# Thresholds of eight pairs through DRAM, weights from another queue, eight score buffers and new task ranks in a fused attention and feed-forward kernel

## The chip, the cores and the metric

One core of one Trainium2 chip. In the profile lines TensorE is PE, VectorE DVE, ScalarE ACT and GpSimd POOL; SP is the engine that here does nothing but issue loads and stores. A load is issued by an engine into that engine's own DMA queue (q1 is SP's, q0 POOL's, q10 ScalarE's). The metric is the device time of one execution in microseconds, as the median of several executions. A ratio is the mean time of one kernel's fast runs over that of the kernel before in the same rounds, so it is not quite the ratio of the medians that stand beside it. The span in a profile is about 2 us shorter than the device time of the same execution.

## The reference

Attention over q, k and v of shape 8 x 8 x 576 x 64 (batch, heads, sequence, head size). A score stays only if it is within `tau` of its row's maximum; the rest is masked:

```python
scores = scale * np.matmul(q, k.transpose(0, 1, 3, 2))
thresh = np.max(scores, axis=-1, keepdims=True) - tau
scores = np.where(scores >= thresh, scores, -1000000000.0)
scores = scores - np.max(scores, axis=-1, keepdims=True)
attn = np.exp(scores)
attn = attn / (np.sum(attn, axis=-1, keepdims=True) + 1e-09)
x = np.matmul(attn, v)
```

Its output, as 4608 tokens of 512, goes through a feed-forward layer: `h = x @ w_in` (512 x 2048), `g = h * sigmoid(1.702 h)`, `g @ w_out` (2048 x 512). The weights arrive in double precision.

## The kernel before

Heads are taken two at a time: 32 pairs, four to a batch, numbered 0 to 31. The feed-forward layer runs in nine blocks of 512 tokens; block 0 needs pairs 0 to 3 and, from its first product on, the converted weights. "hps" is the first product of a block (with `w_in`), "ops" the second (with `w_out`), "ps" are scores, "pv" weighted values, "den" sums. A small list scheduler in the kernel file gives every task an engine, a cost and a rank, and fixes each engine's instruction order when the kernel is built; on the chip every engine runs its list in order.

A 64-bit weight piece (128 x 512) is loaded twice, once shifted by three bytes, into four "stages" in the space of the later `w_out` or into two spare buffers; VectorE and ScalarE turn it into fp32 in four steps:

```python
def load_w(i):                       # 32 pieces, 2 x 512 KB each
    ...
    nc.sync.dma_start(out=t..., in_=dram.bitcast(U32))
    nc.sync.dma_start(out=t3...[:, 0 : 8 * WC - 3], in_=dram.bitcast(U8)[:, 3 : 8 * WC])
...
a = task("SP", 1.1, rank, load_w, i, take=place, lag=5.0)
e = task("DVE", 0.44, rank, cv_ex, i, after=[a])
m = task("ACT", 0.72, rank, cv_power, i, after=[e])
a = task("DVE", 1.14, rank, cv_frac, i, after=[e])
...                                   # and cv_end on DVE
```

A pair's row maxima are reduced on VectorE, lowered by `tau`, and spread over 128 partitions by one wide transpose. They are then subtracted from the scaled scores:

```python
def spread_max(n):
    mb = home(n, "mb", 2 * S, "mb", 1)
    nc.vector.transpose(out=mb, in_=stats[n, ALU.max].unsqueeze(2).to_broadcast([P, 2 * QB, 32]))

def sub(n, t):
    nc.vector.scalar_tensor_tensor(
        out=s, in0=s, scalar=scl, in1=mb, op0=ALU.mult, op1=ALU.subtract)
    # the last 64 keys: two instructions of half the width, one a head

def exps(n, t):
    nc.scalar.activation(out=s, in_=s, func=AF.Exp, bias=shift)
```

Of the kernel before, what the change touches and what calls it, by code (L numbers as in the profile page):

```python
# [19 lines left out]
P = 128  # L20
GELU_SCALE = 1.702
EPS = 1e-9

# [6 lines left out]
def kernel(  # L30
# [48 lines left out]
    work = ctx.enter_context(tc.tile_pool(name="work", bufs=2))  # L79
    psA = ctx.enter_context(tc.tile_pool(name="psA", bufs=3, space=bass.MemoryType.PSUM))  # L80
# [6 lines left out]
    kd = [const.tile([P, P], FP32, name=f"kd{i}") for i in range(2)]  # L87
# [4 lines left out]
    tau_b = const.tile([P, 1], FP32, name="tau_b")  # L92
    scl = const.tile([P, 1], FP32, name="scl")
    shift = const.tile([P, 1], FP32, name="shift")
# [6 lines left out]
    limits = {"psA": 3, "psM": 2, "s_m": 7, "s_t": 2, "io": 3, "xT": 3, "mb": 1,  # L101
              "raw0": 1, "raw1": 1, "qkT0": 1, "qkT1": 1, "v_m": 2, "w64": 2}
# [3 lines left out]

    def task(engine, cost, rank, f, *a, after=(), take=(), give=(), lag=0.06):
        tasks.append((engine, cost, rank, f, a, [x for x in after if x is not None],
                      take, give, lag))
        return len(tasks) - 1  # L110

# [117 lines left out]
    def load_w(i):  # L229
        dst, src, c, j = pieces[i]  # L230
        dram = src[ts(c, P), ts(j, WC)]
        if not wide:
            nc.sync.dma_start(out=dst[:, c, ts(j, WC)], in_=dram)
            return
# [12 lines left out]
        nc.sync.dma_start(out=t.rearrange("p c w -> p (c w)"), in_=dram.bitcast(U32))  # L247
        nc.sync.dma_start(
# [41 lines left out]
    mats, sT, stats, mbs, pss = {}, {}, {}, {}, {}  # L290
# [7 lines left out]
    def prep_kd(n):  # L298
        for h in range(2):
            nc.scalar.copy(  # L300
                out=kd[n % 2][ts(h, D), ts(h, D)], in_=mats[n, 1][ts(h, D), MAIN:S]
            )
# [4 lines left out]
    def scores(n, t, c):  # L307
        qT, kT = mats[n, 0], mats[n, 1]
        ps = psA.tile([P, 2, 512], FP32, name="ps", tag="ps")
        if t == NKT:  # L310
            for i in range(2):
                nc.tensor.matmul(  # L312
                    ps[:, i, 0:SH], lhsT=kd[n % 2], rhs=qT[:, ts(i, SH)],
                    start=True, stop=True,
                )
# [10 lines left out]
    def keep(n, t, c):  # L326
# [3 lines left out]
        else:  # L330
            if c == 0:
                st = home(n, "s_m", 2 * S, "s_m", 7, f"s_m{t}")
                st = st.rearrange("p (h s) -> p h s", h=2)
            else:
                st = sT[n, t]
# [4 lines left out]
    def in_groups(n, t, op):  # L340

        if (n, op) not in stats:
            stats[n, op] = [
                work.tile([P, NKT, 2 * QB], FP32, name="part", tag="part", bufs=2),
                work.tile([P, QB], FP32, name="part_t", tag="part_t", bufs=3),
# [8 lines left out]
    def over_tiles(n, op):  # L354

        pm, pt = stats[n, op]
        r = work.tile([P, 2 * QB], FP32, name="red", tag="red", bufs=3)
# [8 lines left out]
    def over_groups(n, op):  # L366
        r = stats[n, op]
        o = work.tile([64, 2 * QB], FP32, name="fold", tag="fold")
# [4 lines left out]
    def lower(n):  # L373
# [3 lines left out]
            out=f[0:32], in0=stats[n, ALU.max][0:32], scalar1=scl[0:32],  # L377
            scalar2=tau_b[0:32], op0=ALU.mult, op1=ALU.subtract,
# [3 lines left out]
        stats[n, ALU.max] = f  # L382

# [6 lines left out]

    def sub(n, t):
        mb, s = mbs[n], sT[n, t]
        if t < NKT:
            nc.vector.scalar_tensor_tensor(  # L394
                out=s, in0=s, scalar=scl, in1=mb, op0=ALU.mult, op1=ALU.subtract
            )
        else:
            for h in range(2):
                x = s[ts(h, D)]
                nc.vector.scalar_tensor_tensor(  # L400
                    out=x, in0=x, scalar=scl[ts(h, D)], in1=mb[ts(h, D), h, :],
                    op0=ALU.mult, op1=ALU.subtract,
# [6 lines left out]
    def exps(n, t):  # L409
        s = sT[n, t]  # L410
        nc.scalar.activation(out=s, in_=s, func=AF.Exp, bias=shift)  # L411
# [58 lines left out]
    def spread_sums(n):  # L470
# [3 lines left out]
        rc = work.tile([P, S], FP32, name="rc", tag="rc")  # L474
# [35 lines left out]
    def tanh(j):  # L510
        ths[j] = work.tile([P, BLK], FP32, name="th", tag="io", bufs=3)
# [16 lines left out]
    def half(i):  # L528
        osbs[i] = work.tile([P, d_model], FP32, name="osb", tag="io", bufs=3)
# [8 lines left out]
    nc.sync.dma_start(  # L538
        out=tau_b, in_=bass.AP(tensor=tau.tensor, offset=tau.offset, ap=[[0, P], [1, 1]])
    )  # L540
    for t in kd + v_t + [ones_t]:
        nc.gpsimd.memset(t, 0.0)
    nc.gpsimd.memset(ones, 1.0)
    nc.gpsimd.memset(rebias, -896.0 * 2.0**23)
    for h in range(2):
        nc.gpsimd.memset(ones_t[ts(h, D), h, :], 1.0)

    def tau_terms():



        nc.vector.tensor_scalar(
            out=scl, in0=tau_b, scalar1=0.0, scalar2=SCALE, op0=ALU.is_ge, op1=ALU.mult
# [4 lines left out]
        nc.vector.tensor_single_scalar(out=shift, in_=tau_b, scalar=-1.0, op=ALU.mult)  # L558




    FIRST, LAST = -1.0, 1000.0
    BY_PE = 5
    LEAD = 6

    ready_w = []
    for i in range(len(pieces)):
        rank = NPAIR - 0.4 + 0.5 * i / n_in if i < n_in else NPAIR - 0.16 + 0.9 * (i / n_in - 1)
        if not wide:  # L570
            ready_w.append(task("SP", 0.6, rank, load_w, i, lag=2.5))
# [3 lines left out]
        a = task("SP", 1.1, rank, load_w, i, take=place, lag=5.0)  # L575
        e = task("DVE", 0.44, rank, cv_ex, i, after=[a])
        m = task("ACT", 0.72, rank, cv_power, i, after=[e])
# [3 lines left out]
        ready_w.append(task("DVE", 0.72, rank, cv_end, i, after=[a, m] + over, give=place))  # L581

    tau_done = task("DVE", 1.0, -2.0, tau_terms)


# [3 lines left out]
    def feed_forward(blk):  # L589
        b = -(-(blk + 1) * BLK // S) - 1  # L590
        xs = [placed[n] for n in range(NPAIR * (b + 1))]
        for j in range(NFC):
            for p in range(2):
                after = ffn[-1:] + xs[-NPAIR:]
                if blk == 0:
# [3 lines left out]
                    "PE", 1.79, LAST, mm1, blk, j, p, after=after,  # L599
# [4 lines left out]
                "DVE", 0.7, FIRST, gelu, j, after=[a, last_mm2.get(j // 2)],  # L604
                give=("psM", "io"),
            )
        for i in range(BLK // P):
            for p in range(NFC // 2):
                after = ffn[-1:] + [gelus[2 * p], gelus[2 * p + 1]]
                if blk == 0:  # L610
# [3 lines left out]
                    "PE", 1.79, LAST, mm2, i, p, after=after, take=("psM",) if p == 0 else (),  # L614
# [10 lines left out]
    for n in range(NP):  # L625
        gate = per_pair * (n - LEAD)
        after = ffn[gate : gate + 1] if gate >= 0 else []
        r = float(n)
        q0, q1 = (nc.sync, nc.scalar) if n == 0 else (nc.sync, nc.sync)
# [106 lines left out]
```

## Time and profile before

| | us |
|---|---|
| time, median of 3 | 1447.86 |
| span of the profiled run | 1446.5 |
| first hps starts | 115.5 |
| last conversion of `w_out` ends | 216.3 |
| block 1 starts (its first hps) | 304.9 |
| from there to the end | 1141.6 |

The lines that carry this stand in the prediction below. Two more views are needed later. The first is what SP's queue issued in the first 20 us (start, duration, then what is loaded where): four loads of pair 1's q take 2.2 us to issue, its k as long, and the first weight piece comes only after the q and k of pairs 0 to 2.

```profile
6.64 2.20 SPq L189 DMA_DIRECT2D gT<-in_q_dram  x4
8.89 2.12 SPq L189 DMA_DIRECT2D gT<-in_k_dram  x4
...
17.77 0.50 SPq L247 DMA_DIRECT2D w_out<-in_moe_w_in_dram  x1
```

The second is what the DMA queues moved between 10 and 16 us (packets, MB, share of the 16 DMA engines): one queue alone, in packets of some 150 bytes, 0.79 MB in 6 us or 130 GB/s.

```profile
q1 hardware_dynamic: 5148, 0.79, 72.3%
```

### The profile page before, as it was taken

The page shows a single profiled execution, that of the slowest core. Times are in us where ns is not written, and L with a number is a line of the kernel's source. Part 1 is how long each engine was busy: PE and PEld are TensorE (multiplying, and loading weights), DVE is VectorE, ACT ScalarE, POOL GpSimd, SP SyncE. Part 2 cuts the span into 40 slices and gives each one's busy share as a digit, 9 for nine tenths or more (in the row PEclk, how much of TensorE's full clock was granted, in tenths as well). Part 3 has the DMA queues.
Part 4 walks back from the last instruction along what each step waited for, and adds up shares of the span by engine and source line. Part 5 has one row for each costly group of instructions (what it writes and reads, how often), then busy time and mean ns, then how long its engine had stood idle before and what let it go on. Part 6 is the DMA issues. An engine that isn't in the chain of part 4 may idle for free.

```text
span 1446.5 us, 13628 instructions
## 1 busy us (share of the span) xinstructions
PE 1384.0 (96%) x4936; PEld 650.1 (45%) x4936; DVE 997.7 (69%) x1650; ACT 643.6 (44%) x885; POOL 1.3 (0%) x13
## 2 busy tenths in 40 slices
PE   5769979899999999999999999999999999999998
PEld 3334434344444444444444444444444444444443
DVE  7998998888978888888878886788777820200100
ACT  5675544555545554555555554455445500100100
POOL 0000000000000000000000000000000000000000
PEclk8879999999999999999999999999999999999999
DMA  8239461111122012211111111111110000000000
GB/s 240 49 130 287 146 251 40 40 25 25 27 44 49 15 29 39 47 32 25 25 40 39 25 25 39 40 25 21 32 36 16 1 7 22 0 7 22 0 7 22
DMA packets 205074, 72.18 MB, mean 50 GB/s; under 512 B 192208, under 2 KB 192208, under 8 KB 205008
## 3 DMA queue, kind: packets, MB, share of 16 engines
q1 hardware_dynamic: 202640, 71.03, 19.1%
q8 instruction: 39, 0.64, 0.2%
q10 hardware_dynamic: 2368, 0.30, 0.1%
q14 instruction: 27, 0.22, 0.1%
HBM read 61.85 MB, written 9.44 MB: 49 GB/s over the span
## 4 chain that ended last, share of the span: by engine, by line
PE 88%; DVE 8%; ACT 1%; DMA 1%; issue 1%; DVEq 0%; ACTq 0%; SPq 0%
PE ops L523 33%; PE hps L504 31%; PE pv L425 11%; PE ps L319 9%; PE ps L312 2%; PE den L425 2%; DVE part L352 1%; DVE s_m L394 1%; DMA w64s<-in_moe_w_out_dram 1%; DVE mb L386 1%; DVE gT L515 0%; DVE w_out L284 0%; DVE w64s L276 0%; DVE part_t L352 0%; ACT s_m L338 0%
## 5 line engine op out<-in xcount | busy, mean ns | idle before, releaser
L523 PE MATMUL ops<-w_out,gT 128*128 128x512 f32 x1152 | 507.0, 597 | 7.4 <-DVE w_out L284 7.3
L504 PE MATMUL hps<-xT,w_in 128*128 128x512 f32 x1152 | 507.6, 596 | 1.5 <-DVE gT L515 1.4
L352 DVE TRANSPOSE_TENSOR_REDUCE part<-s_m 128x36 f32<-128x1152 f32 x228 | 301.3, 1355 | 107.4 <-ACT s_m L338 106.5
L523 PEld LDWEIGHTS ops<-w_out,gT 128*128 128x128 f32 x1152 | 217.7, 191 | 278.6 <-issue 265.7
L504 PEld LDWEIGHTS hps<-xT,w_in 128*128 128x128 f32 x1152 | 215.3, 190 | 274.2 <-issue 244.4
L515 DVE SCALAR_TENSOR_TENSOR gT<-th,hps 128x512 f32<-128x512 f32 x144 | 97.2, 675 | 226.4 <-ACT th L512 225.8
L338 ACT COPY s_m<-ps 128x576 f32<-128x576 f32 x240 | 137.2, 657 | 144.5 <-PE ps L319 143.3
L407 ACT ACTIVATE s_m<-s_m 128x1152 f32<-128x1152 f32 x120 | 138.4, 1153 | 119.7 <-DVE s_m L394 119.6
L512 ACT ACTIVATE th<-hps 128x512 f32<-128x512 f32 x144 | 85.3, 592 | 229.6 <-PE hps L504 229.5
L394 DVE SCALAR_TENSOR_TENSOR s_m<-s_m,scl,mb 128x1152 f32<-128x1152 f32 x120 | 163.3, 1411 | 0.6
L319 PE MATMUL ps<-qkT 64*128 64x288 f32 x960 | 141.8, 433 | 17.3 <-DVE qkT L295 17.3
L411 ACT ACTIVATE s_m<-s_m,shift 128x1152 f32<-128x1152 f32 x120 | 150.2, 1252 | 2.5
L425 PE MATMUL pv<-s_m,v_m 128*64 128x288 f32 x960 | 126.2, 414 | 0.0
L319 PEld LDWEIGHTS ps<-qkT 64*128 64x128 f32 x960 | 83.2, 190 | 89.4 <-issue 40.4
L530 ACT ACTIVATE osb<-ops 128x512 f32<-128x512 f32 x36 | 21.3, 591 | 220.4 <-PE ops L523 220.4
L425 PEld LDWEIGHTS pv<-s_m,v_m 128*64 128x64 f32 x960 | 67.5, 139 | 64.2 <-issue 15.0
L400 DVE SCALAR_TENSOR_TENSOR s_t<-s_t,scl,mb 64x576 f32<-64x576 f32 x60 | 48.7, 812 | 0.4
L492 DVE TENSOR_TENSOR xT<-pv,rc 128x288 f32<-128x288 f32 (+8 forms) x96 | 28.4, 351 | 22.4 <-PE pv L425 21.1
L352 DVE TRANSPOSE_TENSOR_REDUCE part_t<-s_t 128x18 f32<-128x576 f32 x59 | 43.7, 741 | 0.0
L386 DVE STREAM_TRANSPOSE mb<-thr 128x1152 f32<-128x1152 f32 x30 | 41.3, 1377 | 0.9
L312 PE MATMUL ps<-qkT,kd 128*128 128x288 f32 x120 | 37.1, 432 | 0.0
L425 PE MATMUL pv<-s_t,v_t 128*64 128x288 f32 x256 | 36.5, 406 | 0.0
(66 smaller groups left out, 571.1 us busy)
## 6 DMA issues: line engine op xcount, KB each, us to landing
out_dram<-osb SPq DMA_DIRECT2D x36, 256.0 KB, 2.0
q_raw<-in_q_dram SPq DMA_DIRECT2D x120, 72.0 KB, 2.3
k_raw<-in_k_dram SPq DMA_DIRECT2D x116, 72.0 KB, 2.3
v_m<-in_v_dram SPq DMA_DIRECT2D x64, 128.0 KB, 2.4
w_out<-in_moe_w_in_dram SPq DMA_DIRECT2D x12, 512.0 KB, 6.5
w<-in_moe_w_out_dram SPq DMA_DIRECT2D x12, 512.0 KB, 5.0
w_out<-in_moe_w_in_dram SPq DMA_DIRECT2D x12, 511.6 KB, 7.4
w64s<-in_moe_w_out_dram SPq DMA_DIRECT2D x12, 511.6 KB, 6.0
```

Source lines behind the costliest of these rows:

```text
L312: nc.tensor.matmul(ps[:, i, 0:SH], lhsT=kd[n % 2], rhs=qT[:, ts(i, SH)], start=True, stop=True,)
L319: nc.tensor.matmul(ps[:, h, 0:SH], lhsT=kT[ts(h, D), ts(t, P)], rhs=qT[ts(h, D), ts(c, SH)], start=True, stop=True,)
L338: nc.scalar.copy(out=o, in_=pss.pop((n, t, c))[:, :, 0:SH])
L352: nc.vector.tensor_reduce(out=o, in_=i, axis=AXL.X, op=op, apply_transpose=True)
L394: nc.vector.scalar_tensor_tensor(out=s, in0=s, scalar=scl, in1=mb, op0=ALU.mult, op1=ALU.subtract)
L407: nc.scalar.activation(out=s, in_=s, func=AF.Prelu, alpha=STEEP)
L411: nc.scalar.activation(out=s, in_=s, func=AF.Exp, bias=shift)
L425: nc.tensor.matmul(o[c][ts(h, D), 0:SH], lhsT=lhsT, rhs=rhs, start=(t == 0), stop=(t == NKT),)
L504: nc.tensor.matmul(hidden[j], lhsT=w_in[:, c, ts(j, P)], rhs=xTs[blk][:, c, :], start=(c == 0), stop=(c == NDC - 1),)
L512: nc.scalar.activation(out=ths[j], in_=hidden[j], func=AF.Tanh, scale=GELU_SCALE / 2)
L515: nc.vector.scalar_tensor_tensor(out=gT[j], in0=ths.pop(j), scalar=1.0, in1=hidden.pop(j), op0=ALU.add, op1=ALU.mult)
L523: nc.tensor.matmul(acc[i], lhsT=gT[j][:, ts(i, P)], rhs=w_out[:, j, :], start=(j == 0), stop=(j == NFC - 1),)
```

## The change

Its intent: take work off VectorE, whose queue decides when block 0 gets its inputs. For pairs 0 to 7 the thresholds are no longer spread on VectorE. One small transpose brings them into rows of 32 queries, SP writes them to DRAM and reads them back broadcast over the partitions; the scale moves from the subtraction into the exponential. Weights are loaded from POOL's queue, there are eight score buffers instead of seven (paid for with one `kd`, two io buffers and single small ones), the tau load moves to POOL's queue ahead of the weights, the activation table is loaded first, and each kind of task gets its own rank offset.

```diff
-    limits = {"psA": 3, "psM": 2, "s_m": 7, "s_t": 2, "io": 3, ...
+    limits = {"psA": 3, "psM": 2, "s_m": 8, "s_t": 2, "io": 2, ... "mbt": 1, "row": 1, "kd": 1}
+    EARLY = {"lower_rows": -1.16, "values": 0.42, "exps": 0.63, "load_qk": -0.91, "prep": -1.45,
+             "load_v": 0.65, "over_groups": -1.04, "sub": -0.29}       # pairs 0 to 7
+    LATER = {"in_groups": 0.38}                                        # the others
...
-        nc.sync.dma_start(out=t..., in_=dram.bitcast(U32))             # and the shifted copy
+        nc.gpsimd.dma_start(out=t..., in_=dram.bitcast(U32))
...
+    def lower_rows(n):
+        f, o = flat                                                    # 32 x 64 each
+        nc.vector.tensor_scalar(out=f..., in0=stats[n, ALU.max][0:32]..., scalar1=gap[0:32],
+                                scalar2=None, op0=ALU.subtract)
+        nc.vector.transpose(out=o, in_=f)
+    def row_out(n):
+        nc.sync.dma_start(out=rows[n]..., in_=flat[1][0:QB]...)
+    def row_in(n):
+        nc.sync.dma_start(out=mb, in_=row.to_broadcast([P, 2 * S]))
+        for h in range(2):
+            nc.sync.dma_start(out=mbt[ts(h, D)], in_=row[:, ts(h, S)].to_broadcast([D, S]))
...
-            nc.vector.scalar_tensor_tensor(out=s, in0=s, scalar=scl, in1=mb, ...)
+            nc.vector.tensor_tensor(out=s, in0=s, in1=mb, op=ALU.subtract)
...
-        nc.scalar.activation(out=s, in_=s, func=AF.Exp, bias=shift)
+        nc.scalar.activation(out=s, in_=s, func=AF.Exp, scale=scl, bias=shift)
...
+    BY_DMA = 8
-        rank = NPAIR - 0.4 + 0.5 * i / n_in if i < n_in else ...       # weight pieces
+        rank = 3.61 + 0.42 * i / n_in if i < n_in else ...
-        a = task("SP", 1.1, rank, load_w, i, take=place, lag=5.0)
+        a = task("POOL", 2.4, rank, load_w, i, take=place, lag=5.0)
... (smaller cuts of buffers, an earlier rank for cv_end, and cost estimates of the scheduler, left out)
```

## The prediction

> **What bounds the kernel now.** I read the page first (busy shares, slices), then busy time by stage, then what TensorE waited for, then the costliest groups.
>
> ```profile
> span 1446.5 us, 13628 instructions
> PE 1384.0 (96%) x4936; PEld 650.1 (45%) x4936; DVE 997.7 (69%) x1650; ACT 643.6 (44%) x885; POOL 1.3 (0%) x13
> ...
> PE   5769979899999999999999999999999999999998
> ...
> DVE  7998998888978888888878886788777820200100
> ...
> PEclk8879999999999999999999999999999999999999
> ```
>
> TensorE is the bound over the whole span, but the slices below 9 all lie in the first eight (and the very last). Busy time by stage says where the loss ends (columns: stretch, its length, then busy us of PE, PEld, DVE, ACT, POOL with instruction counts, granted clock, DMA share, GB/s):
>
> ```profile
> 0.00:16.00 16.00, 7.75 (x36) 5.10 (x36) 6.35 (x9) 6.75 (x12) 1.34 (x13) 1.00 0.70 122
> 16.00:41.00 25.00, 15.32 (x100) 8.33 (x100) 23.45 (x42) 16.38 (x22) 0.00 (x0) 0.80 0.93 292
> 41.00:118.00 77.00, 54.46 (x338) 28.81 (x335) 72.22 (x121) 50.63 (x63) 0.00 (x0) 0.82 0.37 115
> 118.00:217.00 99.00, 90.12 (x306) 40.71 (x305) 91.79 (x161) 51.10 (x74) 0.00 (x0) 0.97 0.67 220
> 217.00:305.00 88.00, 78.61 (x327) 38.51 (x326) 72.09 (x119) 46.13 (x63) 0.00 (x0) 0.92 0.20 43
> 305.00:1447.00 1142.00, 1137.70 (x3837) 528.68 (x3835) 731.74 (x1204) 472.65 (x654) 0.00 (x0) 1.00 0.12 25
> ```
>
> After 305 us TensorE is always busy at clock 1.00: nothing done for another engine can shorten that part. All 62 us of idle TensorE, and the slow clock, lie before 305, where VectorE is busy 94% of 16:118 and 93% of 118:217. The waits of TensorE name who was late (total, times, longest):
>
> ```profile
> PE ps L319 <- DVE qkT L295: 17.3, 2, 9.4
> PE den L425 <- ACT s_m L411: 16.9, 2, 9.7
> PE den L425 <- ACT gT L411: 14.5, 2, 10.5
> PE ops L523 <- DVE w_out L284: 7.3, 2, 6.3
> ```
>
> The exponentials (L411) wait for VectorE's subtraction, and the other two lines are VectorE itself: its queue sets when block 0's weights and pairs 0 to 7 are ready. In time order, the first product with w_in (hps) starts at 115.5, TensorE waits for the last w_out piece until 216.4 and for the transposes of pair 8 until 292.6, and block 1 starts at 304.9.
>
> **How much TensorE work lies before block 1.** A product of 128x512 costs two instructions of 0.44 us (507 us over 1152), so 0.88. In the timeline the scores of a pair take 5.5 us, its values 5.0, its sums 4.95. Before block 1 lie 128 products (112.8), scores of nine pairs (49.5), values of eight (40) and sums of five (24.8): 227 us of work in 305 us. The changed order of TensorE has exactly the same list before its first product of block 1. So the change is worth what it moves that one moment: span after = start of block 1 + (1446.5 - 304.9 = 1141.6).
>
> **What the Trainium skill says.** "VectorE: DVE Perf Modes", section on the TRN2 errata, gives an fp32 tensor_tensor as (N+151)/0.96 ns: 1357 ns for 1152 columns, 757 for 576. The trace agrees in form: the 128x288 product with rc takes 452 ns. "DMA: Bandwidth & Descriptors", section "Anatomy of one DMA", puts about 2 us of fixed cost on a transfer; here small loads land in 2.1 to 2.7 us. Its section "Issuing engines are not separate DMA queues" says that all queues run on the same 16 DMA engines and interleave: moving the weights to POOL adds no bandwidth. The trace has one case: q on SP and k on ACT together moved 206 GB/s at 3 to 6 us, one queue alone later some 130, with landing 3.6 us instead of 2.3. "TensorE: Matmul & The Clock Gate", section "What's actually happening", says that idle windows throttle the array; here 18 products after the 6.3 us wait took 10.3 us instead of 7.9.
>
> **The change part by part.** The groups it touches:
>
> ```profile
> L394 DVE SCALAR_TENSOR_TENSOR s_m<-s_m,scl,mb 128x1152 f32<-128x1152 f32 x120 | 163.3, 1411 | 0.6
> L400 DVE SCALAR_TENSOR_TENSOR s_t<-s_t,scl,mb 64x576 f32<-64x576 f32 x60 | 48.7, 812 | 0.4
> L386 DVE STREAM_TRANSPOSE mb<-thr 128x1152 f32<-128x1152 f32 x30 | 41.3, 1377 | 0.9
> ...
> L276 DVE SCALAR_TENSOR_TENSOR w64s<-w,w64s 128x512 int32<-128x512 int32 x16 | 11.1, 694 | 0.5
> ```
>
> Thresholds: a pair now pays on VectorE lower 0.29+0.17+0.18, spreading 1.38, four subtractions of 1.41 and two half tails of 0.81: 9.3 us. After, the first eight pairs pay a row operation 0.29, a 32x64 transpose (estimate 0.22), four tensor_tensor of 1.36 and one tail of 0.76: 6.7. That is 2.6 us a pair, 21 us over eight pairs, and 0.88 MB of broadcast rows a pair instead, with a round trip that I estimate from the landing times above at 0.4+2.3 out and 1.5+4 in: 8 us. The instruction order shows other VectorE work meant to cover it: for pair 0 two transposes and four maxima, 6.9 us.
>
> Weights, conversions: the count stays (32 pieces of 0.42+0.43+0.69+0.69 = 2.2 us). POOL's queue frees SP of 64 issues, and the first six pieces may load from about 4 us on instead of 18 us. The table load of ACT (1.28 us at 7.98) goes ahead of the first data. Eight score buffers let pair 4's scores run before the first hps, in time when TensorE idles.
>
> Now VectorE's queue, as instructions in order times durations from the trace, summed up to three points: placing pair 3 is at 106.5 us of work before and 97.6 after; the last w_out conversion at 205.8 and 200.2; placing pair 7 at 278.9 and 259.4. In the trace of before these three came at 116.6, 216.3 and 300.6, so the queue runs 10 us behind its sum (nearly all of it the first 16 us, when it waits for tau, q and the first copies) and 22 us at pair 7, where it waited for copies that TensorE, stalled, gave late.
>
> After, with the same 10 us: pair 3 is placed at 108 and the first hps follows. TensorE reaches the last w_out pieces after 96 us of work, at about 203, and waits for VectorE until 210.4. From there 64 us of work are left before block 1, plus 2.4 for the slowed clock: 277. Pair 7, at 259.4 plus 10 plus a few us, is placed by 274 and is just not the later one, so the wait of 9.4 us goes. Gain 28 us, of which 6 from the earlier w_out end and the rest from the stall and the work moved ahead.
>
> I take off for the start: POOL's weights compete with q and k of pairs 1 to 3, whose loads kept the DMA busy 80 to 99% of 8 to 18 us, and the row of pair 0 stands on SP behind pair 3's q and k. With loads slowed by 1.3 (206 GB/s shared against 130 alone leaves each 0.8), pair 0's thresholds land near 32 instead of 28 us: VectorE runs some 13 us behind instead of 10. Start of block 1: 280; span 1421.5; time 1.4 above the span as now (1447.86 against 1446.5): 1423. I say 1422.
>
> **Rivals.** (a) Start-up contention is the bound: weights halve the rate of q and k, the row of pair 0 lands at 38, the queue runs 18 us behind; block 1 at 285, time 1428. For it: DMA share 0.93 in 16:41. Against it: a lone small-packet queue does not fill the engines. (b) The round trip is hidden, the start even gains from the earlier table load and unblocked SP; 7 us behind: block 1 at 274, time 1417. (c) The later part suffers: one kd, two io buffers and the delayed later maxima make TensorE wait after block 1. Then some us are added; against it, VectorE has 36% idle after 305. (d) The new order counts on ACT having copies ready; it is busy 66% in 16:118, and 76 us of its work stand before the last exponential of pair 3 (near 100), so a late threshold cannot be caught up there: this adds to (a). (e) Only VectorE's saving counts, without the order: 6 us at the last conversion, time 1442.
>
> **Range and chances.** Two per cent is 1418.9. (b) is below it, my main line and (a) above. Range 1411 to 1434. Faster by over 2%: 0.36, within 2%: 0.61, slower: 0.03 (a race for DMA on every pair, or a broken later part).
>
> **What would show it.** Block 1's first hps near 280 and TensorE at 10 tenths after it; the first hps near 108 to 111; one TensorE wait for the last w_out conversion of 5 to 10 us near 205 to 215, and none of 9 us near 283; the subtraction at 1.36 us; VectorE waiting for the row DMA at pair 0, a few us. I am wrong if TensorE idles after 300, if VectorE waits for weights from POOL for more than 5 us in sum, or if the rows land much later than 8 us after their row operation.

## The result, and the profile after

The changed kernel takes 1435.36 us (median of 4, 1433.01 to 1439.11), the kernel before 1448.16 in the same rounds: a ratio of 0.9914, 95% interval 0.9889 to 0.9938. It is faster by 0.9%, which counts as the same at 2%. The prediction was 1422 with a range of 1411 to 1434: it was 13 us too low, and the result lies just above its range. (That the kernel would be within 2%, its likeliest case at 0.61, came true.) The span of the profiled run is 1431.2 us.

Busy time by stage, with the columns and the stretches that the prediction shows for the kernel before:

```profile
0.00:16.00 16.00, 5.52 (x24) 3.97 (x26) 3.87 (x10) 4.82 (x9) 8.23 (x26) 1.00 0.95 276
16.00:41.00 25.00, 13.59 (x80) 8.74 (x76) 13.80 (x21) 12.43 (x25) 0.00 (x0) 0.80 0.81 198
41.00:118.00 77.00, 59.22 (x405) 31.71 (x402) 72.12 (x127) 61.27 (x74) 8.46 (x16) 0.93 0.50 139
118.00:217.00 99.00, 92.19 (x316) 42.50 (x317) 90.15 (x160) 56.20 (x80) 19.14 (x36) 0.97 0.79 256
217.00:305.00 88.00, 87.77 (x329) 41.23 (x326) 80.33 (x137) 48.95 (x61) 0.00 (x0) 1.00 0.23 60
```

Read the third busy column (VectorE). In 16 to 41 us it was busy for 23.45 of 25 us before and is now busy for 13.80. Of TensorE (first column) the reader sees the opposite at the end: 87.77 of 88 us busy in 217 to 305, where it was 78.61. So the late stall went as predicted, and a hole opened at the start. What VectorE waited for in the first 320 us (total, times, longest) says what made it:

```profile
DVE gT L320 <- DMA gT<-in_q_dram: 11.7, 1, 11.7
...
DVE neg L607 <- DMA tau_b<-in_tau_dram: 6.0, 1, 6.0
...
DVE s_m L447 <- DMA mb<-row: 4.3, 3, 2.1
```

One wait of 11.7 us for the q of pair 1 (`gT` is where pair 1 keeps it). The new order made this load urgent: pair 1's transposes now stand ahead of three of pair 0's maxima (26.6 us, then the maximum at 27.3), where the kernel before had them after pair 0's subtractions (28.3 us). The wait for tau is 6.0 us instead of 3.5, as POOL now issues that load after its memsets; VectorE then waited for pair 0's q anyway, until 9.0. SP's queue shows the same load at its issue, to be held against the two lines of before:

```profile
6.62 15.51 SPq L214 DMA_DIRECT2D gT<-in_q_dram  x4
22.18 4.67 SPq L214 DMA_DIRECT2D gT<-in_k_dram  x4
```

Issuing four loads takes 15.51 us instead of 2.20: the issuing queue itself stands. The DMA queues between 10 and 16 us say why; q0 is POOL's with the weights, q1 is SP's:

```profile
q0 software_dynamic: 488, 2.29, 95.1%
q1 hardware_dynamic: 497, 0.12, 9.6%
```

Both queues moved nearly the same number of packets, and since a weight packet is some 20 times as large, SP's loads got 0.12 MB where they had 0.79 MB before: 6.5 times less. VectorE, held up by pair 1's q, had the row of pair 0 ready only at 35.0 us; SP, held up in the same way and still issuing pair 3's loads, wrote it out at 38.0. Pair 0's first subtraction runs at 43.5 us, where the kernel before has it at 21.3. Only 2.1 us of this were a wait for the row itself.

What TensorE waited for, against the four lines in the prediction:

```profile
PE ps L344 <- DVE qkT L320: 12.2, 3, 10.5
PE den L476 <- ACT s_m L462: 11.5, 4, 5.7
PE ps L344 <- DVE gT L320: 11.1, 1, 11.1
PE ops L574 <- DVE w_out L309: 5.0, 1, 5.0
```

The 9.4 us at 283 are gone; at the start 11.1 us are new, and the wait before the very first product is 10.5 us instead of 7.9. The first hps starts at 117.8 (115.5 before), the last conversion ends at 222.6 (216.3), block 1 starts at 287.55 (304.9).

Two groups of instructions for the costs (count, then busy us and mean ns): the subtraction fell from 1411 to 1351 ns as planned, the exponential rose from 1252 to 1343.

```profile
L462 ACT ACTIVATE s_m<-s_m,shift,scl 128x1152 f32<-128x1152 f32 x120 | 160.5, 1343 | 2.4
L447 DVE TENSOR_TENSOR s_m<-s_m,mb 128x1152 f32<-128x1152 f32 x120 | 156.2, 1351 | 5.0 <-DMA mb<-row 4.3
```

### The profile page after: what moved, and what is told of

The parts are those of the page before. It is cut to its first block, busy times and chain, and to the rows that moved or that the text cites. A ratio compares the mean times of both kernels' runs of the same rounds, so it can differ in the third digit from the quotient of the medians.

```text
span 1431.2 us, 13710 instructions
## 1 busy us (share of the span) xinstructions
PE 1380.6 (96%) x4936; PEld 650.2 (45%) x4936; DVE 970.2 (68%) x1629; ACT 658.9 (46%) x886; POOL 35.8 (3%) x78
## 4 chain that ended last, share of the span: by engine, by line
PE 88%; DVE 6%; SPq 2%; DMA 2%; ACT 1%; issue 1%; DVEq 0%; ACTq 0%
PE ops L574 34%; PE hps L555 34%; PE pv L476 9%; PE ps L344 9%; PE ps L337 2%; SPq L214 2%; DVE s_m L447 1%; DVE part L377 1%; DMA mb<-row 1%; ACT gT L462 1%; ACT gT L458 1%; DMA row<-flat 0%; PE den L476 0%; DVE w_in L309 0%; DVE gT L447 0%
## 5 line engine op out<-in xcount | busy, mean ns | idle before, releaser
L574 PEld LDWEIGHTS ops<-w_out,gT 128*128 128x128 f32 x1152 | 216.2, 190 | 273.8 <-issue 263.5
L555 PEld LDWEIGHTS hps<-xT,w_in 128*128 128x128 f32 x1152 | 216.3, 190 | 267.9 <-issue 256.4
L462 ACT ACTIVATE s_m<-s_m,shift,scl 128x1152 f32<-128x1152 f32 x120 | 160.5, 1343 | 2.4
L447 DVE TENSOR_TENSOR s_m<-s_m,mb 128x1152 f32<-128x1152 f32 x120 | 156.2, 1351 | 5.0 <-DMA mb<-row 4.3
L344 PE MATMUL ps<-qkT 64*128 64x288 f32 x960 | 144.6, 432 | 12.7 <-DVE qkT L320 12.2
L377 DVE TRANSPOSE_TENSOR_REDUCE part_t<-s_t 128x18 f32<-128x576 f32 x59 | 44.2, 749 | 0.7 <-ACT s_t L363 0.2
L543 DVE TENSOR_TENSOR xT<-pv,rc 128x288 f32<-128x288 f32 (+8 forms) x96 | 28.3, 350 | 17.0 <-PE pv L476 15.7
L452 DVE TENSOR_TENSOR s_t<-s_t,mb 64x576 f32<-64x576 f32 x48 | 36.0, 749 | 0.3
L325 ACT COPY kd<-qkT 64x64 f32<-64x64 f32 x60 | 14.5, 241 | 45.6 <-DVE qkT L320 45.2
```

The costliest lines, as they stand in the source:

```text
L344: nc.tensor.matmul(ps[:, h, 0:SH], lhsT=kT[ts(h, D), ts(t, P)], rhs=qT[ts(h, D), ts(c, SH)], start=True, stop=True,)
L377: nc.vector.tensor_reduce(out=o, in_=i, axis=AXL.X, op=op, apply_transpose=True)
L447: nc.vector.tensor_tensor(out=s, in0=s, in1=mb, op=ALU.subtract)
L462: nc.scalar.activation(out=s, in_=s, func=AF.Exp, scale=scl, bias=shift)
L555: nc.tensor.matmul(hidden[j], lhsT=w_in[:, c, ts(j, P)], rhs=xTs[blk][:, c, :], start=(c == 0), stop=(c == NDC - 1),)
L574: nc.tensor.matmul(acc[i], lhsT=gT[j][:, ts(i, P)], rhs=w_out[:, j, :], start=(j == 0), stop=(j == NFC - 1),)
```

## The experiments

Theory S: the large packets of the weights starve the small loads at the start, and the time lost is how late VectorE's queue then runs. The rivals differ by experiment: that POOL's software queue is the culprit and not the packets, that the weights have to come early, that the order of instructions was the difference, or that the terms of the prediction were worth less than it said.

All 17 kernels gave correct results. The groups ran on different chips, on which the kernel before took 1447.0 to 1448.1 us; differences of 1 us between groups mean nothing. Milestones are from the profiled run; "hole" is VectorE's longest wait for a load or a row in the first 100 us other than tau.

| run | time | ratio, 95% interval | first subtraction | hole | last conversion | block 1 |
|---|---|---|---|---|---|---|
| changed kernel | 1435.4 | 0.9914 (0.9889 to 0.9938) | 43.5 | 11.7, q of pair 1 | 222.6 | 287.6 |
| e1 | 1431.0 | 0.9888 (0.9873 to 0.9902) | 30.8 | 7.7, row of pair 1 | 219.9 | 285.1 |
| e2 | 1436.9 | 0.9923 (0.9908 to 0.9938) | 44.2 | 8.7, k of pair 2 | 222.6 | 287.6 |
| e3 | 1437.1 | 0.9935 (0.9918 to 0.9952) | 46.7 | 6.0, k of pair 1 | 225.8 | 290.7 |
| e4 | 1427.5 | 0.9863 (0.9848 to 0.9878) | 27.1 | 11.1, row of pair 1 | 217.8 | 282.7 |
| e5 | 1432.9 | 0.9896 (0.9880 to 0.9913) | 27.0 | 12.1, row of pair 1 | 216.2 | 288.1 |
| e6 | 1431.7 | 0.9887 (0.9872 to 0.9902) | 27.3 | 15.4, row of pair 2 | 221.3 | 286.2 |
| e7 (kernel before) | 1460.9 | 1.0086 (1.0071 to 1.0101) | 35.6 | 16.6, q of pair 0 | 232.0 | 317.5 |
| e8 | 1425.5 | 0.9842 (0.9828 to 0.9857) | 27.6 | 7.9, row of pair 1 | 213.4 | 278.5 |
| e9 | 1431.9 | 0.9889 (0.9875 to 0.9904) | 44.9 | 9.8, q of pair 1 | 221.3 | 286.5 |
| e10 | 1427.5 | 0.9861 (0.9847 to 0.9876) | 27.5 | 12.0, row of pair 2 | 218.3 | 283.3 |
| e11 | 1429.3 | 0.9873 (0.9859 to 0.9888) | 27.1 | none over 1 | 214.0 | 284.2 |
| e12 | 1441.8 | 0.9960 (0.9943 to 0.9976) | 27.4 | 7.3, row of pair 1 | 212.3 | 296.8 |
| e13 | 1421.5 | 0.9821 (0.9806 to 0.9835) | 27.3 | 1.5, a weight piece | 210.7 | 275.6 |
| e14 | 1424.1 | 0.9840 (0.9823 to 0.9857) | 27.3 | 5.0, row of pair 3 | 213.2 | 278.2 |
| e15 | 1459.6 | 1.0083 (1.0068 to 1.0098) | 28.4 | 12.2, row of pair 1 | 232.0 | 309.0 |
| e16 | 1484.4 | 1.0247 (1.0225 to 1.0270) | 38.4 | 9.2, row of pair 0 | 273.2 | 339.5 |
| e17 | 1506.2 | 1.0396 (1.0379 to 1.0413) | 27.4 | 8.1, a weight piece | 297.1 | 363.3 |

### Holding the weights back (e1, e2, e4)

POOL copies one element out of a q/k buffer before it issues its next weight piece, so these pieces cannot start before that load has landed. In e1 and e2 the first piece stays free and the others wait, for pair 3's k and for pair 1's k; the order on the four other engines is the changed kernel's, instruction for instruction. In e4 all pieces wait for pair 3's k, and the scheduler shifts some instructions (e9 tests what such a shift is worth).

```diff
+        kept[n, which] = t                                  # in load_qk
+        if i == FIRST:                                      # in load_w; 1 in e1 and e2, 0 in e4
+            nc.gpsimd.tensor_copy(out=probe, in_=kept[PAIR, 1][:, 0:1])   # PAIR 3, 1, 3
```

> The changed kernel with one thing altered: weight pieces 1 to 31 are loaded only once k of pair 3 has landed (piece 0 still goes at once); every engine's order is the same. Theory S (the weights starve q and k at the start, packet for packet): q of pair 1 lands near 14 to 15 us instead of 26.6, the first subtraction of pair 0 starts near 31 to 34 instead of 43.5, the last w_out conversion ends near 213 instead of 222.6, block 1 starts near 278 to 281 instead of 287.6, time 1422 to 1428. Rival O (the new order with its round trips is what runs late, the loads only hide it): VectorE waits elsewhere instead, block 1 stays at 285 or later, time 1432 or more.

> Same, but the gate opens when k of pair 1 has landed, so that the weights meet q and k of pairs 2 and 3 and the row of pair 0 behind them on the same queue. Theory S: q of pair 1 lands early, then pair 2's q waits for the weights: half the gain or less, first subtraction of pair 0 near 37 to 43, time 1427 to 1434. Rival O: no different from e1.

> All pieces gated until k of pair 3 has landed; the conversion of piece 0 moves later in VectorE's order. Theory S: tau and pair 0's q are no longer slowed either: first transpose near 6.5 us instead of 9.0, so 1 to 3 us better than e1: 1420 to 1426. Rival O: as e1 there, 1432 or more.

Pair 1's q is transposed at 14.3 and 14.8 us in e1 and e2 (26.6 us or later in the changed kernel), so the starvation at that place is gone with the weights. But e1 came out at 1431.0, a few us better than the changed kernel and short of what theory S promised (block 1 at 285.1 fits rival O), and e2 at 1436.9, no better and above its range: the burst of weights, started later, hit the next small transfers. In e2 it was the k of pair 2, in e1 and e4 the row of pair 1. In e4, VectorE's wait and SP's issue of the q ahead of that row:

```profile
DVE gT L451 <- DMA gT<-row: 11.1, 1, 11.1
```

```profile
24.66 13.55 SPq L215 DMA_DIRECT2D q_raw<-in_q_dram  x4
```

The issue of 13.55 us is the same sign as the 15.51 us above, 18 us later. Still, e4 gained 8 us on the changed kernel, 1.5 us short of its range.

### Weights from another hardware queue (e3)

Pieces 1 to 3 are issued from ScalarE's queue instead of POOL's.

```diff
+        queue = nc.scalar if 1 <= i <= 3 else nc.gpsimd
-        nc.gpsimd.dma_start(...)                            # both copies of the piece
+        queue.dma_start(...)
```

> The changed kernel with weight pieces 1 to 3 issued from ACT's hardware queue at the start instead of POOL's. Theory S: any second queue with 4 KB packets starves the small ones, so q of pair 1 still lands at 22 us or later and the time stays within 1432 to 1440. Rival Q (POOL's software queue is served first, or its descriptor writing disturbs): q of pair 1 lands before 18 us, time 1424 to 1430.

The time is 1437.1 us, no better. Three queues were then at work between 10 and 16 us:

```profile
q0 software_dynamic: 319, 1.46, 59.8%
q10 hardware_dynamic: 250, 0.90, 37.5%
q1 hardware_dynamic: 322, 0.08, 6.4%
```

Again the small loads (q1) move as many packets as POOL's queue and nearly nothing in bytes. But this run is no clean test. POOL's queue still carried 1.46 MB in that window, and the time was hurt in another way: ScalarE's own work began only at 20.3 us, behind the issues of its weight loads, so that VectorE waited 11.1 us for its copies. What decides is a later window, 20 to 28 us, in which POOL's queue is empty and ScalarE's carries the weights:

```profile
q10 hardware_dynamic: 552, 2.04, 75.9%
q1 hardware_dynamic: 1478, 0.18, 14.9%
```

There SP's issue of pair 1's k took 7.80 us instead of 2.12, so weights on a hardware queue starve the small loads too: it is not POOL's software queue alone. They starve them less, though; the small queue moved 2.7 times as many packets as the weights' queue. Why is open.

For the even counts beside POOL's queue there is a likely source. The Trainium skill says in "DMA: Bandwidth & Descriptors", section "Queues, rings and completion order", that each DMA engine takes turns between the queues that have work, packet by packet. The trace fits that beside POOL's queue (488 to 497 packets, and 319 to 322), and not in the window just shown (552 to 1478). The page's packet is a group of some 9 to 17 descriptors (entries of a queue's list), while the small packets that the profile counts have 0.24 KB on average, about one row of q (256 bytes); that the two words mean the same unit is not shown. What the page does not draw is the consequence for a queue of small packets.

### Weights back on SP (e5), and the kernel before with its weights on POOL (e7)

e5 is the changed kernel with the loads in SP's queue; e7 is the kernel before with only these loads moved to POOL's. In both the scheduler also shifts instructions on the other engines.

```diff
-        nc.gpsimd.dma_start(...)      ->  nc.sync.dma_start(...)      # e5, in load_w
-        task("POOL", 2.4, rank, load_w, ...)  ->  task("SP", 1.1, rank, load_w, ...)
                                                            # e7: the same the other way round
```

> The changed kernel with the weight pieces issued from SP's queue again, where they stand in the order of the tasks: the q and k of pairs 0 to 3 and pair 0's row of thresholds come ahead of the first piece, six pieces (twelve transfers, some 6 MB) stand ahead of pair 1's row. Theory S (the big packets of a second queue starve the small ones; how soon the weights themselves come does not matter): q of pair 1 is transposed before 13 us, the first subtraction of pair 0 runs before 30 us (43.5 in the changed kernel); pair 1's row, behind six pieces in its own queue, is then late by 8 to 14 us, so block 1 starts at 278 to 285 and the time is 1423 to 1431. Rival R (the weights have to come early, which is what POOL's queue was for): the first subtraction is early but the conversions are late by as much, block 1 starts no sooner than 287 and the time is 1434 or more.

> The kernel before, with only the weight loads moved to POOL's queue. Theory S: the same starvation of q and k of pair 1 as in the changed kernel, its first use on VectorE after 22 us instead of about 7 to 10, VectorE's queue 5 to 15 us later from there on, block 1 at 308 to 318 and the time 1450 to 1460. Rival R (weights early are a gain by themselves): the wait of 9.4 us at the end of block 0 of the kernel before shrinks and the time is 1438 to 1445.

e7 shows the loss without the thresholds, the buffer and the rank offsets: 1460.9 us, 12.7 us slower than the kernel before, just above what was expected, with one wait of 16.6 us for a q where there had been 2.4. It is pair 0's q here, and not only pair 1's as expected: the weights start early enough to starve the very first load. The shifted order does not explain it: up to that wait VectorE's order is that of the kernel before, and the first subtraction is already 14.3 us late. e5 missed its time by 2 us: the start is early, but six pieces in SP's own queue stand ahead of pair 1's row, which is waited for 12.1 us, and later pieces wait behind SP's other business so that TensorE waits 9.3 us for one of them. e7 also holds a comparison of packet sizes. Its small packets are half as large as the changed kernel's (0.13 KB on average, not 0.24), and between 10 and 16 us

```profile
q0 software_dynamic: 471, 2.23, 96.2%
q1 hardware_dynamic: 471, 0.06, 6.9%
```

the count is again that of the weights, and the bytes are half: 0.06 MB, not 0.12. That is what turns by packet mean.

So neither queue is right by itself; in one queue the small load is behind the burst, in two it is starved by it.

### Holding all weights back until a row has landed (e6, e8)

As e4, but behind the row of pair 1 (e6) or of pair 0 (e8) instead of a k. The order on the four other engines is the same in both.

```diff
+        kept[n] = mbt                                       # in row_in
+        if i == 0:                                          # in load_w
+            nc.gpsimd.tensor_copy(out=probe, in_=kept[1][:, 0:1])   # e6; kept[0] in e8
```

> The changed kernel, all weight pieces held back (POOL copies one element of it first) until pair 1's row of thresholds has landed. The order on SP and on TensorE is that of the run with the gate behind pair 3's k. Theory S: the wait of 11.1 us for pair 1's row in that run goes, the first subtractions of pairs 0 and 1 run before 29 and 46 us, the first piece lands after 42 us; if the conversions that then come late do not hold VectorE's queue for more than 5 us, block 1 starts at 273 to 280 and the time is 1417 to 1425. Rival R (the weights must come early): VectorE waits over 6 us for the first piece, block 1 starts at 282 or later and the time is 1426 or more, no better than the gate behind pair 3.

> As the gate behind pair 1's row, but behind pair 0's row: pieces from about 27 us. Theory S: between the gate behind pair 3's k (1427.5) and the gate behind pair 1's row, with pair 1's row still late by 6 to 11 us: 1422 to 1428, block 1 at 278 to 283. Rival R: the earlier weights make it the better of the two gates on rows.

e8 came out in its range at 1425.5 us, e6 at 1431.7 not at all, so that e8 is the better of the two, as the rival had it: its numbers were right and its reason was wrong. In e6, pair 1's row was on time and VectorE waited only 2.6 us for weights, but then 15.4 us for the row of pair 2:

```profile
DVE s_m L451 <- DMA mb<-row: 15.4, 1, 15.4
```

```profile
51.60 9.96 SPq L215 DMA_DIRECT2D q_raw<-in_q_dram  x4
61.67 6.74 SPq L215 DMA_DIRECT2D k_raw<-in_k_dram  x4
...
78.49 0.46 SPq L432 DMA_DIRECT2D row<-flat  x1
```

VectorE had that row ready at 63.3 us. SP issued it at 78.5, because it stood for 27 us in the issues of pair 4's q and k (17 us of them) and of the v behind them, which the burst starved. A starved load thus also holds what stands behind it in the queue that issues it.

### The order alone (e9), and spacing by two rows (e10)

e9 has e8's order, instruction for instruction, without the one-element copy, so its weights start at 2.5 us again. e10 puts pieces 0 and 1 behind pair 0's row and the rest behind pair 1's.

```diff
-        if i == 0:
-            nc.gpsimd.tensor_copy(out=probe, in_=kept[0][:, 0:1])          # e9
+    GATES = {0: 0, 2: 1}                                    # e10: piece -> pair whose row it waits for
+        if i in GATES:
+            nc.gpsimd.tensor_copy(out=probe, in_=kept[GATES[i]][:, 0:1])
```

> The order of the run with the gate behind pair 0's row, instruction for instruction on TensorE, VectorE, ScalarE and SP, but without POOL's one-element copy, so the weights start at 2.5 us as in the changed kernel. Theory S (the time of the loads counts): SP's issue of pair 1's q takes 10 us or more again, pair 0's first subtraction runs after 40 us, block 1 starts at 285 to 290, the time is 1433 to 1439. Rival O (the slightly other order on VectorE was the gain of the gates): 1424 to 1427, as with the gate.

> Pieces 0 and 1 held back until pair 0's row has landed, pieces 2 and on until pair 1's; the order on the other engines is that of the gate behind pair 0's row. Theory S: pair 1's row then meets two pieces (some 2 MB, 6 us) and not six, its wait on VectorE falls from 7.9 to under 3 us, and q and k of pair 4 are issued after the first six pieces have landed, in under 6 us; block 1 starts at 270 to 276 and the time is 1415 to 1421. Rival R (each spacing only moves the starved load on): another small load is late by 5 us or more, block 1 at 276 to 283, 1422 to 1430.

e9 took 1431.9 us, 6.4 more than e8, with intervals that do not touch: what e8 gains comes from the time of the loads, not from its slightly other order. (It is a little below both the expected range and the changed kernel, whose own runs spread over 6 us.) e10 did not come out: 1427.5, in the rival's range. The row of pair 1 is waited for only 2.3 us, as theory S said, but the burst then met q and k of pair 4 (issues of 6.1 and 5.3 us) and the row of pair 2 (12.0 us). Up to here each spacing had only moved the collision.

### Three gaps (e13, e14)

From e10's trace: the first three conversions run before pair 2's row goes out, the next three after pair 3's. So one piece can go behind pair 0's row, two behind pair 1's and everything else behind pair 2's. e14 takes two and two instead. The order on the other four engines is e8's in both.

```diff
-    GATES = {0: 0, 2: 1}
+    GATES = {0: 0, 1: 1, 3: 2}                              # e13; e14: {0: 0, 2: 1, 4: 2}
```

> Piece 0 goes behind pair 0's row, pieces 1 and 2 behind pair 1's, pieces 3 and on behind pair 2's; instruction for instruction the order of the gate behind pair 0's row (1425.5) on TensorE, VectorE, ScalarE and SP. Theory S: pair 1's row meets one piece, no row is waited for longer than 2.5 us, q and k of pair 4 are issued in under 5 us; the last conversion ends 6 to 9 us earlier than in that run (212.7), block 1 starts at 269 to 274 (278.5), the time is 1414 to 1419. Rival R (each spacing moves the starved load on): a later row or load is late by 5 us or more, 1422 to 1430.

> As e13, with pieces 0 and 1 behind pair 0's row, 2 and 3 behind pair 1's, 4 and on behind pair 2's. Theory S: pair 1's row still meets two pieces and is waited for 2 to 3 us, as in the run with two and four; pair 2's row is not; 1 to 3 us above e13, 1416 to 1421. Rival R: 1422 to 1430.

e13 is the best kernel: 1421.5 us, a ratio of 0.9821 to the kernel before (the interval reaches from 0.9806 to 0.9835, so over 1.6% faster), and all its runs lie within 0.5 us. It is 2.5 us above what was expected of it, and its rows are waited for 0.7 us. The two stages of the start, against those of the changed kernel above:

```profile
0.00:16.00 16.00, 7.32 (x34) 5.18 (x35) 6.50 (x13) 6.45 (x12) 1.88 (x14) 1.00 0.93 134
16.00:41.00 25.00, 19.73 (x128) 11.08 (x128) 24.36 (x38) 22.30 (x33) 2.40 (x3) 0.93 0.68 159
```

VectorE is busy 24.36 of 25 us where it was busy 13.80, and TensorE 19.73 where it was 13.59. e14 fell into the rival's range: 1424.1, with 6.7 us of waits for rows; its interval overlaps those of both e8 and e13.

### What the other terms are worth (e11, e12, e15)

Each undoes one part on top of e8 (1425.5): thresholds through DRAM only for pair 0, seven score buffers, no rank offsets.

```diff
-    BY_DMA = 8
+    BY_DMA = 1                                              # e11
-    "s_m": 8
+    "s_m": 7                                                # e12, and in the pool
-    EARLY = {...};  LATER = {"in_groups": 0.38}
+    EARLY = {};  LATER = {}                                 # e15
```

> On top of the gate behind pair 0's row (1425.5): the thresholds of pairs 1 to 7 are made on VectorE again (spread_max), only pair 0's go through DRAM. The prediction's sum: 7 pairs x 2.6 us = 18 us more work in VectorE's queue of block 0; the wait of 7.9 us for pair 1's row goes; block 1 starts 5 to 12 us later than with the gate alone, 1430 to 1438. Rival T (the thresholds through DRAM give back in waits what they save in work): 1420 to 1428.

> On top of the gate behind pair 0's row (1425.5): seven score buffers instead of eight. If the eighth buffer is worth what the prediction gave it (2 to 4 us between pairs, where TensorE waits for a buffer): 1427 to 1431. If the row trips hide it or the order shifts: within 1 us of 1425.5.

> On top of the gate behind pair 0's row (1425.5): the ranks by kind of task are emptied, so a pair's tasks all keep the pair's rank. If the ranks do what the prediction took the new order for (work moved ahead of the first hps and later maxima delayed): the first hps moves by 3 us or more and the time is 1429 to 1442. If the thresholds, the buffers and POOL's queue are all: within 2 us of 1425.5.

The thresholds are worth 3.9 us there, less than expected: VectorE has 17 us more work, but it no longer waits 7.9 us for a row, and the last conversion ends only 0.6 us later. The loss comes after it, in the stretch before block 1 (70.2 us instead of 65.1). The eighth buffer is worth 16.4 us, four times the most that was expected (the 2 to 4 us stood in the expectation alone; the prediction had put no number on the buffer by itself). The last conversion is as early as in e8; between it and block 1 lie 84.5 us instead of 65.1. TensorE's waits after 200 us in e12:

```profile
PE ops L578 <- DVE w_out L312: 12.1, 2, 6.2
PE pv L480 <- ACT s_m L466: 6.1, 2, 3.3
```

The second line is new (e8 has only one wait there, 4.7 us for a weight). It is TensorE at 279 to 288 us waiting for the exponentials of the last pair before block 1, the place where the kernel before lost its 9.4 us. Without the eighth buffer more of the pairs' work is left at the end. The ranks are worth 34 us, of which 3.4 come after block 1 has started. Without them two rows are waited for 23.3 us in sum and the first hps starts at 149.9 us. These three numbers must not be added up: each part was taken out of an order in which the others, the weights' ranks too, were tuned to it.

### Smaller weight packets (e16, e17)

The counts above suggest a direct test: the same bytes in packets of 1 KB instead of 4. Each load is cut in two with gaps between its runs; the order on the other four engines is the changed kernel's (e16) and e13's (e17).

```diff
+        def cut(ap, y):
+            return ap.rearrange("p (x y e) -> p y x e", x=2, y=2)[:, y]
+        for y in range(2):
+            nc.gpsimd.dma_start(out=cut(t..., y), in_=cut(dram.bitcast(U32), y))
                                                            # and the shifted copy likewise
```

> The changed kernel with each weight load cut into two loads of 1-KB packets instead of one of 4-KB packets, weights from 2.5 us on as before; the order on the other four engines is the changed kernel's. Theory S (the DMA engines take turns by packet): between 10 and 16 us both queues still move about equally many packets, but q and k get 0.3 to 0.6 MB instead of 0.12; SP's issue of pair 1's q takes 4 to 9 us (15.5), pair 0's first subtraction runs at 30 to 38 us (43.5), block 1 starts at 276 to 285 (287.6), the time is 1421 to 1432. Rival Q (POOL's queue is preferred, or the shares go by bytes or by time): SP's issue still takes over 12 us, the subtraction runs after 41 us, the time is 1433 or more.

> The spacing of e13 (1421.5) with weight packets of 1 KB. Theory S: what collisions are left there (SP's issue of pair 4's q took 3.2 us, pair 3's row out took 6.6 us, VectorE waited 6 us for weight pieces) get milder for the small transfers and longer for the weights: 1418 to 1423. Rival Q: the same time within 1 us if the packet's size does not matter; above 1425 if 1-KB packets make the weights themselves late.

The small loads got their share back: SP's issue of pair 1's q took 4.3 us instead of 15.5, q1 moved 0.53 MB between 10 and 16 us instead of 0.12, and the first subtraction came at 38.4. But the test failed as a test of the packets' size. POOL waited for earlier halves before it issued the next, probably because the cut halves overlap for the framework:

```profile
POOL w_out L280 <- DMA w_out<-in_moe_w_in_dram: 44.4, 8, 7.0
```

The weights moved only 0.76 MB in these 6 us instead of 2.29, and their packets in the record have 3.4 KB on average, not 1. Fewer weights in flight would have relieved the small loads as well. And the weights were now late, 31 us of waits in one line of VectorE alone, so both kernels are slower than the kernel before (1484 and 1506 us); for e17 the rival had said so. It shows the other side of the bargain: weights this slow cost more than the starvation did.

## Why the prediction was wrong, point by point

The step that failed is the one that begins "I take off for the start": "With loads slowed by 1.3 ... pair 0's thresholds land near 32 instead of 28 us: VectorE runs some 13 us behind instead of 10." SP's loads moved 6.5 times less in the same 6 us, the first subtraction that needs the row ran at 43.5, and VectorE ran 22.4 us behind its sum (last conversion at 222.6). The sum itself was right: predicted 200.2 us of work up to that conversion, and the durations in the trace add up to 200.2. The 1.3 came from one case in the trace of before, two queues of equally small packets. It was wrong against packets some 20 times as large, beside which SP's queue kept its share by packet and lost it by bytes. The load that this held up was also another: the prediction watched the row behind pair 3's loads, while the wait was for pair 1's q. Rival (a) had the mechanism and sized it at a half (row at 38, 18 us behind, 1428); its counter-argument, "a lone small-packet queue does not fill the engines", was beside the point.

Three readings in the prediction were wrong without carrying the miss. The DMA was busy 77% of 8 to 18 us, not 80 to 99%. Of the 62 us of idle TensorE 59 lie before 305, the rest after it. The 18 "products" that took 10.3 us are 18 instructions, nine products by its own count. Of its signs of being wrong, TensorE did not idle after block 1 and VectorE waited for no weights; pair 0's row was used 9.0 us after its row operation instead of 8. So the signs would not have found the fault.

- **One moment carries the change:** right. In the changed kernel and in e1 to e6 and e8 to e14, whose block 1 starts anywhere from 275.6 to 296.8 us, the span ends 1143.6 to 1143.7 us later (e13: 275.6 and 1419.2; e12: 296.8 and 1440.4). The prediction had 1141.6; why the new order takes 2.0 us longer there is open.
- **From the last conversion to block 1:** the prediction had 64 us plus 2.4 for the slowed clock; it is 64.9 to 65.2 in the changed kernel and in e1, e2, e3, e4, e6, e8, e9, e10, e13 and e14.
- **The lag:** the prediction put block 1 at 277 for a lag of 10 us and at 280 for 13. e13 has 10.5 and 275.6, e8 has 13.2 and 278.5. With the right lag the sum gives block 1 to within 2 us. At 22.4 us it gives 287 to 289, and 287.55 was measured.
- **VectorE's saving:** right. Subtraction 1351 ns (estimated 1357), row operation and small transpose 0.23 us each (0.29 and 0.22), and 17 us of VectorE's work back in e11 for seven pairs, 2.4 each.
- **The wait of 9.4 us before block 1 goes:** right. The eighth buffer, which the prediction named only in passing, has a part in it: without it (e12) 6.1 us of waits come back at this place, for exponentials and not, as before, for pair 8's transposes.
- **Not seen:** exponentials of 1343 ns instead of 1252 with the scale in a pointer. The Trainium skill has it ("ScalarE: Activation LUTs", section "What ACT_TABLE_LOAD costs": a [128,1] pointer operand adds about 93 ns); measured 91. It was overlooked; ScalarE has room.
- **Rival (c)**, TensorE idle later: it is busy for all of 305 to 1420 us (1115.0 of 1115).

The 13.4 us from 1422 to 1435.4 are 7.6 from block 1 (287.55 against 280), 2.0 from the stretch after it, 1.4 from the step from span to time (1.8 measured, 0.4 in the prediction, which had taken 1.4 from a median and another run's span and then rounded 1423 down to 1422), and 2.4 from the profiled run's being the fastest of four. That e13 ends at the predicted 1422 is luck: its block 1 is 4.4 us earlier than predicted, and the other two terms take that back.

**What is shown:** moving the same loads in time, with all other engines' orders fixed, moves the time by 10 us (e9 to e13); moving them to POOL in the kernel before costs 12.7 us. **Shown beside POOL's queue:** where both queues had work throughout, they moved equal numbers of packets (488 and 497, 475 and 475 in the changed kernel; 483 and 484 in e9; 471 and 471 in e7, with small packets of half the size). **Not shown:** that packets of another size in the weights' queue would change the shares; the run that was to do this (e16) changed the rate too, and its counts were 226 and 4250. **Open:** why ScalarE's queue starves less than POOL's (e3), and the 2.0 us after block 1.

## What to carry to other kernels

Before moving a bulk load to a queue of its own, compare packet sizes: a stream of small packets beside it can lose most of its bandwidth (here 0.12 MB were left of 0.79), and the engine that issues the small loads then stands (15.51 us for 2.20), with all that is behind them. Ask also which small load a new order makes urgent. Let bulk loads go in the gaps between the small transfers that the critical path needs, with a data dependency and not by the queue's order alone, and look after each move at which small transfer the burst meets now. And undo the parts of a tuned change one at a time before believing which of them carries it: here the transfer of the thresholds, its most visible part, was worth 4 us, and the buffer and the ranks several times that.

## What the Trainium skill lacked or had wrong

- "DMA: Bandwidth & Descriptors", section "Queues, rings and completion order", has the turns by packet but not what they mean for a queue of small packets: beside packets of 4.7 KB on another queue, packets of 0.24 KB were as many (497 against 488 in 6 us) and got 0.12 MB of 2.41 MB, where alone SP's queue had moved 0.79. Beside ScalarE's queue the counts were not equal (1478 small ones against 552 in 8 us, e3), which the section does not account for.
- The same page, section "Issuing engines are not separate DMA queues", does not say that a starved queue makes the issuing instructions stand: four issues on SP took 15.51 us instead of 2.20, and a finished row waited 15 us behind such issues (e6).
- No page gives the round trip of a small row through DRAM, out and back broadcast to 128 partitions: in the changed kernel, for pair 0, 1.7 us out and 3.8 us in.
